# Attention and MLP on one core: the second MLP product by seven block products for a pair of token tiles

## The chip, the cores and the metric

The kernel runs on 1 core of one Trainium2 chip. The metric is device time in microseconds for one execution; the median of 3 runs of the kernel before is 604.26 us (603.35 to 604.57). Engines are named as in the profile: PE (matmul), PEld (weight load of a matmul), DVE (VectorE), ACT (ScalarE), POOL (GpSimd), SP (the queue that issues most DMAs). Lines "L674" are lines of the kernel before; "after L774" is a line of the changed one.

## What is computed

```python
def rmsnorm(x, g): return x / np.sqrt(np.mean(x * x, axis=-1, keepdims=True) + 1e-06) * g
# q, k, v: (8, 12, 448, 64)
q_n, k_n = rmsnorm(q, g_q), rmsnorm(k, g_k)
attn = softmax(q_n @ k_n^T / 8)               # per batch and head
x = concat_heads(attn @ v)                    # (8, 448, 768)
xn = (x - mean) / sqrt(var + 1e-06) * g_ln
out = x + relu(xn @ w_ch1) @ w_ch2            # 768 -> 3072 -> 768, no biases
```

## The kernel before

**Tiles.** A batch has 448 tokens. Tiles 0 to 2 hold 384 of them (128 each). The 64 tokens that are left over from two batches form one more tile, which is worked on with the odd batch. So the MLP of an even batch has three token tiles and that of an odd batch four. Activations and weights are fp16, sums fp32 in PSUM. Both weight matrices (`sh.w1`, `sh.w2`) stay in SBUF.

**The MLP** (`mlp_chunks`). The *up* product, 24 chunks of hidden features f: six matmuls (L658) of one 128x128 weight block against all the batch's tokens at once (384 or 512 columns), and one Relu on ACT (L660) into `hT[f]`. The *down* product, for every token tile and each half of the 768 output columns: 24 matmuls (L674) with a block of `hT` as the weights and 384 columns of `w2` as the moving data, in four chunks of six; then one DVE instruction (L678) multiplies by the token's 1/std (`rs`) and adds x, and the tile is stored. The last tile of the last batch takes its second half as two pieces of 192 columns. Norm scale 1/std commutes with Relu, so it is applied at the end.

**Attention** goes in 48 head pairs, 7 steps each. A step has one score matmul (L359, 448 columns; L365 for the left-over tokens), one Exp on ACT (L377) into an `E` tile, and the value matmuls (L414, L416) of the pair before. Two pairs form a *unit* (`UNITS`), whose q, k, v are loaded together (`load_unit`, L128 and L136) and prepared by `pieces`: squares on ACT (L218), their sums on DVE (L221), Ln and Exp for 1/rms (L224, L225), k times gains on POOL (`kg`, L235), its high half on ACT (`khi`, L243) and low half on DVE (`klo`, L246), q scaled on DVE (`qn`, L68), v cast on POOL (L291, L297). From unit 8 on, eight DMA transposes on SP (L264 to L277) bring k and q into `kU` and `qU`; `kU` has two buffers, so a unit's transposes wait for the last score of the unit two before.

**What sets the order.** Batch 0's attention follows the hand-written `ORDER`. From then on `run_rest` walks the MLP chunks of batch b and, after each chunk, emits as many attention steps of the next batch as its share of the cost asks for (42 steps, all done 13 chunks before the MLP's end). Inside those last 13 chunks, `ln_list` emits the next batch's layer norm: statistics, `norm` on DVE (L603), and a DMA transpose per tile on SP into `xnT` (L630). PE, ACT, POOL and SP run in this emitted order; DVE's order is chosen by the scheduler. Each engine works strictly through its own queue.

**Buffers that the change touches.** Loads: two buffers for all of q, k, v of a unit (`p_in`). Exp outputs: one buffer for an even pair (7 tiles), one for an odd pair (6) and one for the left-over tile. `xnT` and `hT` hold all 512 columns. PSUM: three banks shared by up and down (`ps_m`, tag "mlp"), two and later three for scores.

Of the kernel before, what the change touches and what calls it, by code (L numbers as in the profile page):

```python
# [55 lines left out]
RS_LO, RS_HI = 2.0 ** -2 / XS, 2.0 ** 12 / XS  # L56
# [20 lines left out]
class _Fast:  # L77


    def __init__(self, ctx, tc, sh, q, k, v, gs, g_ln, w1, w2, out):  # L80
        self.gs, self.g_ln = gs, g_ln
        self.tc, self.nc, self.sh = tc, tc.nc, sh
        self.q, self.k, self.v, self.w1, self.w2, self.out = q, k, v, w1, w2, out
        nc = tc.nc
        pool = lambda name, bufs, **kw: ctx.enter_context(tc.tile_pool(name=name, bufs=bufs, **kw))
        self.p_in = pool("p_in", 2)
        self.p_n = pool("p_n", 2)
        self.p_e = pool("p_e", 1)
# [22 lines left out]
        self.hT = fix.tile([128, NFF, 512], FP16, name="hT", tag="hT")  # L111
# [26 lines left out]
    def load_first(self):  # L138
        nc = self.nc
        flat = self.hT.rearrange("p f n -> p (f n)").bitcast(FP32)  # L140
# [29 lines left out]
    def load_unit(self, u):  # L170
        nc = self.nc
        b, hs, m = UNITS[u]
        t = self.p_in.tile([128, 3, 14, D], FP32, tag="qkv", name="qkv")
        eng = self.nc.sync if u < 11 else self.nc.gpsimd
        for n in (1, 0, 2):
            self.load_main(nc.gpsimd if u == 10 and n == 2 else eng, n, t[:, n, 0:6 * m], b, hs, 2 * m)
            self.load_left(eng, n, t[:, n, 6 * m:7 * m], b, hs, 2 * m)
        self.loads[u] = [t[:, n] for n in range(3)]
# [13 lines left out]
    def pieces(self, u):  # L192
# [9 lines left out]
        def begin():  # L202
            c["t"] = self.loads.pop(u)
            c["ssq"] = self.p_n.tile([128, 2, 14], FP32, tag="ssq", name="ssq")[:, :, 0:g]
            c["rt"] = self.p_n.tile([128, 2, 14], FP32, tag="rt", name="rt")[:, :, 0:g]
# [6 lines left out]
        def square(n):  # L212

            o = c["khl" if n == 1 else "qn"].rearrange("p g e d -> p (g e d)").bitcast(FP32)
            if u == 0 and n == 1:
                o = self.hT.rearrange("p f n -> p (f n)").bitcast(FP32)[:, 5376:5376 + g * D]
# [128 lines left out]
    def scores(self, p, i):  # L345
# [5 lines left out]
        if i == 0:  # L351
            k = 7 - p % 2
            c["E"] = self.p_e.tile([128, k, S], FP16, tag=f"E{k}", name="E")
# [17 lines left out]
        for d, x in enumerate(ps):  # L371
            if i < 6 or (p + d) % 2 == 0:
                o = c["E"][:, i]
            else:
                o = self.prs[p + d]["EL"] = self.p_e.tile([128, S], FP16, tag="EL", name="EL")
# [18 lines left out]
    def values(self, p, i):  # L394
        nc = self.nc
        c = self.prs[p]
        E = c["EL"] if i == 6 and p % 2 else c["E"][:, i]
# [95 lines left out]
    def attention(self):  # L493
# [3 lines left out]
        for u in range(4, nu):  # L497
# [4 lines left out]
            pieces = ["bai", "d", "c", "e", "j", "gv", "k", "l", "m", "w", "x", "y"]  # L502
# [5 lines left out]
            if u < nu - 2 and f"L{u + 2}" not in done:  # L508
                todo.setdefault(e + (8 if u == DMA_UNIT else 1), []).append(
                    lambda u=u: self.load_unit(u + 2))  # L510
            last = e
            for x, names in enumerate(pieces):
# [71 lines left out]
    def ln_ops(self, b):  # L584
# [14 lines left out]
        def norm(t):  # L599

            c["xn", t] = self.p_m.tile([128, DM], FP16, tag="xn", name="xn", bufs=4)
# [16 lines left out]
    def ln_list(self, b):  # L618
        ops = self.ln_ops(b)
        n = len(self.tok_tiles(b))  # L620
        call = lambda *names: lambda: [ops[x]() for x in names]
        return [call("A", "N0", "N1", "X0", "N2", "X1", *(["N3"] if n > 3 else []), "X2",
                     *(["X3"] if n > 3 else []), "R")]

    def ln_trans(self, b, xn, t):
        nc, sh = self.nc, self.sh
        if t == 0:
            self.xnT = self.p_m.tile([128, NDC, 512], FP16, tag="xnT", name="xnT")
        if b:
            nc.sync.dma_start_transpose(self.xnT[:, :, ts(t, 128)], xn)  # L630
            return
# [15 lines left out]
    def mlp_chunks(self, b):  # L647

        nc, sh = self.nc, self.sh
        tiles = self.tok_tiles(b)  # L650
        n = len(tiles)
        N = 128 * n
        xnT, hT = self.xnT, self.hT

        def up(f):
            ps = self.ps_m.tile([128, 512], FP32, tag="mlp", name="psH")
            for dc in range(NDC):
                nc.tensor.matmul(ps[:, 0:N], sh.w1[:, dc, ts(f, 128)], xnT[:, dc, 0:N],  # L658
                                 start=(dc == 0), stop=(dc == NDC - 1))
            nc.scalar.activation(out=hT[:, f, 0:N], in_=ps[:, 0:N], func=AFT.Relu)  # L660

        cur = {}
        order = [(t, g) for g in ((0, 384), (384, 384)) for t in range(n)] if b == 0 else [
            (t, g) for t in range(n) for g in (
                ((0, 384), (384, 192), (576, 192)) if (b, t) == (B - 1, n - 1)
                else ((0, 384), (384, 384)))]

        def down(t, g, s):
            cols = slice(g[0], g[0] + g[1])
            if s == 0:  # L670
                cur["ps"] = self.ps_m.tile([128, 512], FP32, tag="mlp", name="psC")
            ps = cur["ps"]
            for f in range(6 * s, 6 * s + 6):
                nc.tensor.matmul(ps[:, 0:g[1]], hT[:, f, ts(t, 128)], sh.w2[:, f, cols],  # L674
                                 start=(f == 0), stop=(f == NFF - 1))
            if s == 3:
                x = tiles[t]
                nc.vector.scalar_tensor_tensor(  # L678
                    out=x[:, cols], in0=ps[:, 0:g[1]], scalar=self.rs[:, b, t:t + 1],
                    in1=x[:, cols], op0=ALU.mult, op1=ALU.add)  # L680
                if t == n - 1:
                    self.store(b, t, cols, nc.scalar if b == B - 1 else nc.sync)
                elif cols.stop == DM:
                    self.late.append((b, t, slice(0, DM)))
            elif s == 1:
                for a in self.late:
                    self.store(*a)
                self.late = []

        for f in range(0 if b else UP_FIRST, NFF):  # L690
            yield 6 * N / 2.4, (lambda f=f: up(f))
        for t, g in order:
            for s in range(4):
                yield 6 * g[1] / 2.4, (lambda t=t, g=g, s=s: down(t, g, s))

    def up_first(self, t):
# [5 lines left out]
        for f, ps in enumerate(self.psU):  # L702
# [4 lines left out]
            if t == 2:  # L707
                nc.scalar.activation(out=self.hT[:, f, 0:384], in_=ps[:, 0:384], func=AFT.Relu)
# [26 lines left out]
    def run_rest(self):  # L735
        steps, mark, upto = self.steps, self.mark, self.upto
        tail = 13
        for b in range(B):
            chunks = list(self.mlp_chunks(b))
            total = sum(c for c, _ in chunks)  # L740
            if b + 1 == B:
                for i, (_, emit) in enumerate(chunks):
                    if i == len(chunks) - 40:
# [6 lines left out]
            done, items = 0.0, None  # L750
            for i, (cost, emit) in enumerate(chunks):
                if items and len(chunks) - i <= len(items):
                    items.pop(0)()
                emit()
                done += cost
# [9 lines left out]
    def flag(self):  # L765
# [5 lines left out]
        good = self.p_m.tile([128, n], FP32, tag="xn", name="good", bufs=4)  # L771
        cnt = self.fix.tile([128, 3], FP32, name="cnt", tag="cnt")
# [13 lines left out]
        nc.vector.tensor_reduce(out=cnt[:, 2:3], in_=good[:, 0:nr], axis=AX.X, op=ALU.add)  # L786
        nc.vector.tensor_reduce(out=cnt[:, 0:1], in_=cnt, axis=AX.X, op=ALU.add)
        ps = self.ps_o.tile([1, 1], FP32, tag="oB", name="psF")
        nc.tensor.matmul(ps, sh.ones, cnt[:, 0:1], start=True, stop=True)
        nc.vector.tensor_scalar(out=sh.flag, in0=ps, scalar1=128.0 * (n + nk + nr) - 0.5, scalar2=None,  # L790
# [3 lines left out]
def _general(tc, sh, q, k, v, g_q, g_k, out):  # L794

    nc = tc.nc
    P1, NS = 112, 4
# [108 lines left out]
def kernel(  # L906
# [19 lines left out]
    sh.warm = const.tile([128, 1], FP32, name="warm")  # L926
# [5 lines left out]
    sh.gmax = const.tile([128, 1], FP32, name="gmax")  # L932
# [13 lines left out]
    with tc.If(val > 0, label="general"):  # L946
        _general(tc, sh, q, k, v, g_q, g_k, out)
# [30 lines left out]
```

## Time and profile before

| what | us |
|---|---|
| median of 3 runs | 604.26 |
| the profiled execution, device time | 604.66 |
| its span | 603.0 |
| PE busy | 577.6 |
| ACT / DVE / POOL busy | 358.5 / 287.8 / 184.8 |
| first matmul / start of the last matmul, from the span's start | 5.26 / 598.81 |
| MLP of batch 1: first up, first down, end | 123.0, 162.8, 200.0 |
| MLP of batch 2: first up, first down, end | 200.0, 232.9, 261.6 |
| MLP of batch 7: first up, first down | 536.3, 567.6 |

The span is the time from the first to the last recorded instruction; the device time is 1.7 us longer. A matmul's own duration in the profile includes its way through the array, and the next one starts long before it ends, so costs on PE are read here from the spacing of starts: a run of matmuls in the chain of work divided by their number. Granted clock is 0.996 over the span and 1.00 in every later stage, so spacings of different stages can be compared.

### The profile page before, as it was taken

How to read it: one execution, taken by the hardware profiler on the slowest of the kernel's cores; microseconds unless marked ns; L12 is line 12 of the kernel's file. 1: busy time of each engine (PE TensorE's matmuls, PEld its weight loads, DVE VectorE, ACT ScalarE, POOL GpSimd, SP SyncE). 2: the span in 40 equal slices, each digit the busy share in tenths (PEclk: the TensorE clock that was granted, in tenths of full speed). 3: DMA queues.
4: the chain of work that ended last, by engine and by line, in shares of the span. 5: the costliest groups of instructions: out<-in, count | busy, mean ns of one | idle time of the engine just before them, and what ended most of it. 6: DMA issues, size and time to landing. Idle time of an engine off the chain costs nothing.

```text
span 603.0 us, 11494 instructions
## 1 busy us (share of the span) xinstructions
PE 577.6 (96%) x4502; PEld 341.9 (57%) x4502; DVE 287.8 (48%) x645; ACT 358.5 (59%) x673; POOL 184.8 (31%) x246
## 2 busy tenths in 40 slices
PE   2877999999999999999999999999999999999997
PEld 1555566654566666655566666655556666654565
DVE  5798567734256255724256255642355422450011
ACT  5996887359743598548755498537765287114300
POOL 3844432232642345423542245505322000000000
PEclk9899999999999999999999999999999999999999
DMA  7999999574957578947866386848533330040011
GB/s 209 281 196 206 207 222 197 106 212 86 146 130 125 106 126 155 170 121 122 120 127 131 104 125 153 165 120 152 114 68 88 92 62 1 27 106 1 1 53 54
DMA packets 130285, 75.18 MB, mean 125 GB/s; under 512 B 96500, under 2 KB 120420, under 8 KB 130228
## 3 DMA queue, kind: packets, MB, share of 16 engines
q1 hardware_dynamic: 113092, 44.50, 37.7%
q0 software_dynamic: 16192, 29.30, 22.9%
q8 instruction: 36, 0.59, 0.4%
q10 hardware_dynamic: 944, 0.62, 0.3%
q14 instruction: 21, 0.17, 0.1%
HBM read 52.30 MB, written 11.01 MB: 105 GB/s over the span
## 4 chain that ended last, share of the span: by engine, by line
PE 88%; ACT 2%; DVE 2%; issue 0%; DVEq 0%
PE psC L674 36%; PE psH L658 35%; PE psS L359 8%; PE oA L414 5%; PE oB L416 2%; PE psS L365 1%; ACT E L377 1%; PE tr L322 0%; ACT khl L218 0%; PE psU L704 0%; DVE stat L582 0%; ACT hT L660 0%; PE tr L336 0%; DVE xn L603 0%; DVE x L431 0%
## 5 line engine op out<-in xcount | busy, mean ns | idle before, releaser
L658 PE MATMUL psH<-xnT,w 128*128 128x512 f16 (+1 forms) x1134 | 242.1, 353 | 0.0
L674 PE MATMUL psC<-w,hT 128*128 128x384 f16 (+1 forms) x1368 | 234.8, 324 | 0.0
L377 ACT ACTIVATE E<-psS,rr_all 128x448 f16<-128x448 f32 x312 | 193.5, 635 | 49.5 <-PE psS L359 48.6
L660 ACT ACTIVATE hT<-psH 128x512 f16<-128x512 f32 (+1 forms) x189 | 104.0, 550 | 130.9 <-PE psH L658 128.8
L674 PEld LDWEIGHTS <-hT 128*128 128x128 f16 x1368 | 127.2, 98 | 78.8 <-issue 4.3
L658 PEld LDWEIGHTS <-w 128*128 128x128 f16 x1134 | 102.3, 98 | 83.3 <-issue 2.9
L359 PE MATMUL psS<-qU,kU 128*128 128x448 f16 x288 | 101.3, 358 | 8.7 <-ACT E L377 5.8
L414 PEld LDWEIGHTS <-E 128*128 128x128 f16 x936 | 65.0, 99 | 44.3 <-issue 5.0
L235 POOL TENSOR_TENSOR qkv<-qkv,gprod 128x896 f32<-128x896 f32 x21 | 43.7, 2079 | 95.8 <-issue 51.7
L414 PE MATMUL oA<-v,E 128*128 128x65 f16 x864 | 66.9, 194 | 0.1
L678 DVE SCALAR_TENSOR_TENSOR x<-psC,rs_all,x 128x384 f32<-128x384 f32 x48 | 29.2, 616 | 78.4 <-PE psC L674 77.9
L128 POOL DMA_DIRECT2D qkv<-in_k_dram x14 | 11.1, 793 | 137.0 <-ACT E L377 64.3
L416 PE MATMUL oB<-v,E 128*128 128x65 f16 x288 | 52.1, 194 | 0.1
L429 DVE RECIPROCAL rec_all<-oA 128x6 f32<-128x6 f32 x48 | 9.3, 194 | 88.2 <-PE oA L414 87.8
L221 DVE TENSOR_REDUCE ssq<-khl 128x14 f32<-128x896 f32 (+1 forms) x24 | 25.6, 1065 | 44.6 <-ACT khl L218 44.5
L359 PEld LDWEIGHTS <-kU 128*128 128x128 f16 x288 | 28.2, 99 | 25.9 <-issue 6.0
L221 DVE TENSOR_REDUCE ssq<-qn 128x14 f32<-128x896 f32 (+1 forms) x25 | 26.2, 1046 | 21.8 <-ACT qn L218 21.7
L68 DVE SCALAR_TENSOR_TENSOR qn<-qkv,rr_all 128x256 f16<-128x256 f32 (+1 forms) x72 | 26.4, 426 | 18.1 <-ACT rr_all L225 18.1
L416 PEld LDWEIGHTS <-E 128*128 128x128 f16 x312 | 30.3, 97 | 0.2 <-DVE xl L436 0.2
L431 DVE TENSOR_TENSOR x<-oA,rec_all 128x384 f32<-128x384 f32 x48 | 26.8, 558 | 1.5
L582 DVE BATCH_NORM_STATS2 stat<-x 128x6 f32<-128x256 f32 (+1 forms) x75 | 26.0, 404 | 0.6
L246 DVE TENSOR_TENSOR khl<-qkv,khl 128x896 f16<-128x896 f32 x21 | 22.7, 1079 | 4.0 <-ACT khl L243 3.9
(114 smaller groups left out, 447.3 us busy)
## 6 DMA issues: line engine op xcount, KB each, us to landing
out_dram<-x SPq DMA_DIRECT2D x20, 384.0 KB, 2.5
qkv<-in_v_dram POOLq DMA_DIRECT2D x15, 384.0 KB, 6.5
qkv<-in_k_dram POOLq DMA_DIRECT2D x14, 384.0 KB, 3.9
qkv<-in_q_dram POOLq DMA_DIRECT2D x14, 384.0 KB, 5.4
w<-in_moe_w_ch_dram POOLq DMA_DIRECT2D x3, 1536.0 KB, 13.0
w<-in_moe_w_ch_dram POOLq DMA_DIRECT2D x2, 2304.0 KB, 24.8
qkv<-in_k_dram SPq DMA_DIRECT2D x7, 384.0 KB, 5.7
qkv<-in_q_dram SPq DMA_DIRECT2D x7, 384.0 KB, 6.0
```

The lines of the kernel that those rows point to most:

```text
L68: nc.vector.scalar_tensor_tensor(out=out, in0=x, scalar=8.0, in1=r.unsqueeze(2).broadcast_to([x.shape[0], g, D]), op0=ALU.mult, op1=ALU.mult)
L221: nc.vector.tensor_reduce(out=c["ssq"][:, n], in_=c["sq", n], axis=AX.X, op=ALU.add)
L235: (nc.vector if u in DVE_KG else nc.gpsimd).tensor_tensor(out=c["t"][1], in0=c["t"][1], in1=sh.gprod.unsqueeze(1).broadcast_to([128, g, D] ...
L359: nc.tensor.matmul(ps[0][:, 0:S], c["main"][:, ts(i, 128)], c["q"][:, ts(h, S)], start=True, stop=True)
L377: nc.scalar.activation(out=o, in_=x[:, 0:S], func=AFT.Exp, scale=self.units[u][3][:, g:g + 1], bias=EXP_BIAS)
L414: nc.tensor.matmul(oA[:, t, cs], E[:, ts(t, 128)], rhs, start=(i == 0 and t == 0), stop=(i == 6 and t == 2))
L416: nc.tensor.matmul(oB[:, cs], E[:, 320:448], rhs, start=(i == 0), stop=(i == 6))
L431: nc.vector.tensor_tensor(out=x[:, :, 128 * hp:128 * hp + 128].rearrange("p t (e d) -> p t e d", e=2), in0=oA[:, :, :, 0:D], in1=rec[:, 0: ...
L658: nc.tensor.matmul(ps[:, 0:N], sh.w1[:, dc, ts(f, 128)], xnT[:, dc, 0:N], start=(dc == 0), stop=(dc == NDC - 1))
L660: nc.scalar.activation(out=hT[:, f, 0:N], in_=ps[:, 0:N], func=AFT.Relu)
L674: nc.tensor.matmul(ps[:, 0:g[1]], hT[:, f, ts(t, 128)], sh.w2[:, f, cols], start=(f == 0), stop=(f == NFF - 1))
L678: nc.vector.scalar_tensor_tensor(out=x[:, cols], in0=ps[:, 0:g[1]], scalar=self.rs[:, b, t:t + 1], in1=x[:, cols], op0=ALU.mult, op1=ALU.add)
```

## The change

**Down product.** Batch 0 keeps the plain product. From batch 1 on, tiles are taken in *groups*: pairs [0,1] and [2,3] in odd batches, [2] and then [0,1] in even ones. For a pair, the down product is a 2x2 block product (two token tiles; two halves of f; two halves of the output columns), done in the Strassen-Winograd form: seven products of 12 matmuls with 384 columns, numbered "1" to "7", in place of eight. DVE makes the sums of `hT` blocks: three instructions of 512 fp16 elements for every four f and their partners (`sums`), and one of 1536. The sums of weight blocks (`w2s`, T1, T2, T4) are made once on DVE, beside the end of batch 0 and the start of batch 1, and T3 = B12 - B22 replaces B12 in `w2`; a single tile uses T3 too, with one more sum. Partial results go to x by more DVE adds (`add`), by a copy of product 1 to SBUF on ACT, and, except in batch 7, by three ACT multiplications with `rs` and three POOL additions (`join`).

**Up product.** It runs per group too: 256 columns for a pair (two f share a PSUM bank and a Relu), 128 for a single tile (four f). `xnT` holds one group, in one buffer: the second group's transposes are emitted once the first group's up product has been.

**Loads and exp tiles.** q, k and v have one buffer each; the next unit's k, q or v is loaded as soon as the present unit's `klo`, `qn` or left-over v cast has read its own. Units 5 and 7 are loaded into idle parts of other buffers. `khi` and `klo` move ahead of q's square in `pieces`. Exp tiles come from one ring of 9.

**Safety.** The final check (`flag`) tests also that the scales of two tiles of a pair are within a factor of 4; otherwise the general path runs, which loads half of `w2` again.

```diff
-        self.p_in = pool("p_in", 2)
+        self.p_in = pool("p_in", 1)
...
+        t = self.loads.setdefault(u, [None] * 3)
+        for n in which:
+            t[n] = flat[:, n] if flat is not None else self.p_in.tile(
+                [128, 14, D], FP32, tag="qkv"[n], name="qkv"[n])
...
-            pieces = ["bai", "d", "c", "e", "j", "gv", "k", "l", "m", "w", "x", "y"]
+            pieces = (["bai", "d", "c", "e", "j", "gv", "k", "l", "m", "w", "x", "y"]
+                      if u <= DMA_UNIT else
+                      ["bai", "d", "j", "k", "c", "e", "gv", "l", "m", "w", "x", "y"])
...
+                for y in set(names) & set("klw"):
+                    if DMA_UNIT <= u < nu - 1:
+                        todo.setdefault(at + 1, []).append(
+                            lambda u=u, t={"k": 1, "l": 0, "w": 2}[y]: self.load_unit(u + 1, (t,)))
...
-            c["xn", t] = self.p_m.tile([128, DM], FP16, tag="xn", name="xn", bufs=4)
+            c["xn", t] = self.p_m.tile([128, DM], FP16, tag="xn", name="xn", bufs=2)
...
+            if t in (0, 2):
+                self.xnT = self.p_m.tile([128, NDC, 256], FP16, tag="xnT", name="xnT")
+            nc.sync.dma_start_transpose(self.xnT[:, :, ts(t % 2, 128)], xn)
...
+    def mlp_group(self, b, tiles, end):
...
+        def up(f):
+            ps = self.ps_m.tile([128, k, N], FP32, tag="mlp", name="psH")
+            for i in range(k):
+                for dc in range(NDC):
+                    nc.tensor.matmul(ps[:, i], sh.w1[:, dc, ts(f + i, 128)], self.xnT[:, dc, 0:N],
+                                     start=(i == 0 and dc == 0), stop=(i == k - 1 and dc == NDC - 1))
+            nc.scalar.activation(out=hT[:, f:f + k], in_=ps, func=AFT.Relu)
...
+        def sums(i):
+            f, f2 = slice(4 * i, 4 * i + 4), slice(HALF + 4 * i, HALF + 4 * i + 4)
+            if n == 1:
+                tt(S1[:, f], A1(f), A1(f2), ALU.add)
+                return
+            tt(S1[:, f], A2(f), A2(f2), ALU.add)
+            tt(S2[:, f], S1[:, f], A1(f))
+            tt(A2(f), A2(f), A1(f))
...
+        p = run("1", A1(lo), B11)
+        yield p[0]
+        yield 0, lambda: sums(2)
+        yield p[1]
+        yield add("1", 0, 0)
+        yield from run("2", A1(hi), B21)
+        yield add("2", 0, 0)
+        yield 0, lambda: tt(A1(hi), A1(hi), S2)
+        yield late
+        yield from run("6", S2, T2)
+        p = run("5", S1, T1)
+        yield p[0]
+        yield 0, lambda: nc.scalar.copy(out=U, in_=bank["1"])
+        yield p[1]
+        yield 0, lambda: tt(U, U, bank["6"], ALU.add)
+        yield 0, lambda: tt(V, U, bank["5"], ALU.add)
...
+        yield from run("7", A2(lo), T3)
+        yield add("7", 1, 1)
+        yield add("7", 1, 0)
+        if not last:
+            for out, x, t in ((U, U, 1), (W, V, 0), (V, V, 1)):
+                yield 0, lambda out=out, x=x, t=t: nc.scalar.activation(
+                    out, x, AFT.Copy, scale=self.rs[:, b, t0 + t:t0 + t + 1])
+            yield join(V, 1, 1)
...
+        yield from run("3", A1(hi), B22)
...
+            yield from run("4", A2(hi), T4)
...
+        for i, x in enumerate(self.mlp_group(b, first, False)):
+            yield x
+            if i % 2 and i // 2 < len(second):
+                yield 0, ln[f"N{second[i // 2]}"]
+            if i == ups - 1:
+                for t in second:
+                    yield 0, ln[f"X{t}"]
+        yield from self.mlp_group(b, second, True)
+
+    def groups(self, b):
+        return ([0, 1], [2, 3]) if b % 2 else ([2], [0, 1])
```

More of the change, by code (lines that the diff above doesn't have):

```diff
@@ L507, in attention @@
                 continue
[L508 to L510 removed]
+            if u == DMA_UNIT - 2:
+                todo.setdefault(e + 1, []).append(lambda u=u: self.load_unit(u + 2))
             last = e
@@ L657, in up @@
             for dc in range(NDC):
-                nc.tensor.matmul(ps[:, 0:N], sh.w1[:, dc, ts(f, 128)], xnT[:, dc, 0:N],
+                nc.tensor.matmul(ps[:, 0:384], sh.w1[:, dc, ts(f, 128)], xnT[:, dc],
                                  start=(dc == 0), stop=(dc == NDC - 1))
-            nc.scalar.activation(out=hT[:, f, 0:N], in_=ps[:, 0:N], func=AFT.Relu)
+            nc.scalar.activation(out=hT[:, f], in_=ps[:, 0:384], func=AFT.Relu)
         cur = {}
[L663 to L666, printed above, removed]
@@ L690, in mlp_chunks @@
[L690 to L694, printed above, removed]
+                self.add(0, t, g, ps)
+                if g and t < 2:
+                    self.late.append((0, t, slice(0, DM)))
+                elif t == 2:
+                    self.store(0, t, slice(g * HCOL, g * HCOL + HCOL))
+            elif s == 1:
+                self.store_late()
@@ new lines, in first_mlp, with store_late, add @@
+        for f in range(UP_FIRST, NFF):
+            yield 6 * 384 / 2.4, (lambda f=f: up(f))
+        for g in range(2):
+            for t in range(3):
+                for s in range(4):
+                    yield 6 * HCOL / 2.4, (lambda t=t, g=g, s=s: down(t, g, s))
+    def store_late(self):
+        for a in self.late:
+            self.store(*a)
+        self.late = []
+    def add(self, b, t, g, ps, c0=0, c1=HCOL):
+        x = self.tok_tiles(b)[t][:, g * HCOL + c0:g * HCOL + c1]
+        self.nc.vector.scalar_tensor_tensor(
+            out=x, in0=ps, scalar=self.rs[:, b, t:t + 1], in1=x, op0=ALU.mult, op1=ALU.add)
@@ L754, in run_rest @@
                 emit()
+                if cost and (i > 33 if b == 0 else b == 1) and ops:
+                    ops.pop(0)()
                 done += cost
```

214 lines of the change are left out of this document (156 added, 58 removed).

## The prediction

> **What bounds the kernel now.** I read the page's busy shares first, then the stretches of single batches, then PE's waits, and last the chain of work in order of time. In the stretch table (columns: stretch; total us; busy us of PE, PEld, DVE, ACT, POOL; clock; DMA share; GB/s) the rows are batch 2 up to the end of its attention steps, its last 13 chunks, and then the waits of PE after 100 us:
>
> ```profile
> PE 577.6 (96%) x4502; PEld 341.9 (57%) x4502; DVE 287.8 (48%) x645; ACT 358.5 (59%) x673; POOL 184.8 (31%) x246
> ```
> ```profile
> 199.96:248.93 48.97, 48.79 (x428) 30.33 (x427) 24.73 (x60) 40.19 (x79) 27.34 (x37) 1.00 0.79 141
> 248.93:261.55 12.62, 12.62 (x80) 7.58 (x79) 9.00 (x18) 2.14 (x5) 0.69 (x3) 1.00 0.73 153
> ```
> ```profile
> PE psS L359 <- ACT E L377: 0.4, 2, 0.2
> ```
>
> PE is busy throughout at full clock, and after 100 us it waits 0.4 us for others in all. So after 100 us the time is what PE is given, and a matmul's price is its spacing. The chain in order of time (start, us, what) gives spacings from unbroken runs:
>
> ```profile
> 55.81 2.01 PE psU L704 x36
> 110.40 12.78 PE psC L674 x78
> 540.49 27.30 PE psH L658 x126
> 567.79 31.27 PE psC L674 x216
> ```
>
> 128 columns: 2.01/36 = 55.8 ns, each matmul with a weight load of its own. 384 columns: 12.78/78 = 163.8 ns. 512 columns: 27.30/126 = 216.7 ns. These lie on a line of 0.419 ns a column, which gives 109.4 ns for 256 columns, a width that the trace does not show. The last row fits too: its 48 matmuls of 192 columns leave 83 ns each.
>
> **PE's work, step by step.** The built order gives the counts. Batch 0 is unchanged.
> 1. Up, batches 1 to 7. Before: 576 x 216.7 + 432 x 163.8 = 195.6 us. After: 11 pairs x 144 = 1584 of 256 columns, 173.3 us, and 3 single tiles x 144 = 432 of 128 columns, 24.1 us: 197.4. Cost 1.8 us.
> 2. Down. A pair needs 84 matmuls in place of 96; 11 x 12 = 132 fewer x 163.8 ns = 21.6 us gained. Single tiles keep 48. The last pieces of 192 columns stay.
> 3. Scores, values and transposes keep their counts.
> Net -19.8 us. From the profiled execution's 604.66 this gives 584.9, if nothing new waits. That execution is 0.4 us above the median of the runs, so 584.5 is the floor beside the median.
>
> A weight load reads 98 ns as a mean, but in the psU run 36 of them pass at 55.8 ns each, so I price short matmuls by spacing. The Trainium skill speaks against the narrow up product: the page TensorE: Matmul & The Clock Gate, Back-to-back issue gap, puts a sustained stream of weight loads and matmuls at about 81 ns for 128 columns. By that figure the single tiles would cost 432 x 25 ns = 10.9 us more; the psU row, at 55.8 ns with weight loads, is against it, and it stays out of the sum.
>
> **Work beside PE.** None of these is on the path while the engine keeps up.
> 4. ACT. Relus: 150 of 512 columns at 600 ns = 90 us in place of 93.5. New: 11 copies and 27 scalings of 384 columns; an xnT copy of 384 columns took 0.48 us, so 38 x 0.48 = 18 us. 358 becomes 373 of 585 us.
> 5. DVE. An fp16 sum of two fp16 tiles is not in the trace. From above: `klo`, the only wide two-input SBUF form, took 618 ns at 448 and 1075 at 896 elements, so 683 ns at 512, 1.73 us at 1536, 1.34 us at 1152. From below: an fp16 copy of 896 took 393 ns, so no less than some 0.25 us at 512. I take the upper price, from the row that is nearest in form. A pair then adds 9 x 0.68 + 1.73 + four more adds x 0.616 = 10.3 us, a single tile 2.0, the 16 weight sums 21 us: 11 x 10.3 + 6 + 21 = 140. DVE goes from 288 to 428 of 585 us, 73%. Batch 2's stretch above has 33.7 us of DVE work in 61.6; with 12.3 more it is at 46 in 60.
> 6. POOL. 27 additions of 384 elements at 2079 x 384/896 = 0.89 us: 24 us more, 209 of 585. `load_unit` of units 9 and 10 leaves SP for POOL, nine issues of 0.60 to 0.80 us each.
> 7. Buffers. In `ORDER`, the values that free each of the nine ring tiles stand ahead of the score that wants it, on PE's own queue; no new wait, 0. The first 100 us, where most of the present waits are, keep their path.
>
> The Trainium skill, VectorE: DVE Perf Modes, gives fp16 tensor_tensor two elements a cycle at 0.96 GHz (section on auto-detection); an estimate from it is 0.27 us plus the fixed part for 512, about 40% under item 5. No row here shows it; it changes no term below.
>
> **New waits, and what hides them.**
> 8. The second group's transposes. They follow the eight transposes of a unit on SP, which is in order. In an odd batch there is room: the unit's transposes are released by step 5 and SP is free before the first group's up product ends; two transposes need 1.24 + 2.8 us (issue, landing) against 13.8 us of products. In an even batch it is tight. SP before, batch 2:
>
> ```profile
> 206.77 2.63 SPq L264 DMA_TRANSPOSE kU<-khl  x1
> 209.45 4.76 SPq L267 DMA_TRANSPOSE kU<-khl  x2
> 214.31 3.83 SPq L274 DMA_TRANSPOSE qU<-qn  x3
> 218.19 2.51 SPq L277 DMA_TRANSPOSE qU<-qn  x2
> ```
> The start is 6.8 us after the batch's first matmul, the end 13.9 us later; in batches 4 and 6 it took 12.5 and 11.6, at best anywhere 10.6. After: step 5 is emitted behind four up chunks (24 x 55.8 = 1.34 us each; a step costs one score of 0.19 and four values of 0.03, 0.31 us), so release is at 4 x 1.34 + 5 x 0.31 + 0.2 = 7.1 us, SP is free at 17.7 to 21.0, and the second transpose has landed 4.0 us later, at 21.7 to 25.0. PE reaches the pair's up product after 6 x 1.34 + 8 x 0.98 + 20 x 0.31 = 22.1 us. Wait 0 to 2.9 us in each of three batches; I take 1.2, a unit between the best and batch 6: **+3.6 us** (0 to 8.7).
> 9. Product "6" reads S2. Between the last up matmul and it lie 24 matmuls, 3.9 us. Needed: Relu 0.60 and two sums 1.37. That leaves 1.9 us for DVE's queue. In DVE's built order a square sum (L221, 1.08 us) that waits for ACT stands between these two sums in the first pair of odd batches. So the wait is 0 mostly, up to 1.1 us; I take 0.2 x 11 pairs = **+2.2 us** (0 to 12). PSUM banks: each is freed one product (1.97 us) or more ahead of its next use, against an add of 0.62; 0.
> 10. `khi` now follows `kg` by two steps, and POOL may still issue loads: an even batch's unit has about 15 us, in which POOL has 9.6 us of own work and waits for `qn`. ACT may then stand up to 2 us, with Exps and Relus queued behind it; three score banks and three up banks let PE run on for about that long. I take 0; it is the start of rival C.
>
> Sum: 604.66 - 19.8 + 3.6 + 2.2 = 590.7; beside the median 590.3. A difference under 0.2% (1.2 us) is what a measurement of this kernel cannot tell from no change.
>
> **The rivals.**
> A. All is hidden: 584.5. For it: PE's 0.4 us of waits now, and the room in items 4 to 6. Against: item 8's tight sum. Chance 0.22.
> B. DVE's queue holds up most pairs: each pays 0.7 to 1.1 us at product "6", "7" or the next bank, 8 to 12 us: 598 to 602, with item 8 in it. For it: 46 us of 60 in even batches, in one order. Chance 0.14.
> C. Slower: the single load buffer. k's load now waits for `klo`, and the next unit's chain for the load. The ring is load 2.0 us of issue and 3.9 of landing, `kg` 2.08, `khi` 0.96, `klo` 1.08: 10.0 us of the 15 us that an even unit has; odd units have 20. Each of four hand-overs waits behind what its queue holds (POOL for `qn`, ACT and DVE about 1 us each). If these waits pass 5 us the unit's transposes are late and PE stands at the scores. It decides against the change once each of the 9 even units loses (604.3 - 590.3)/9 = 1.6 us; at 2 us each 608. Against it: the chain has 11 steps between `klo` and the transposes' release. Chance 0.09.
> D. Short matmuls are held by their weight loads: at 98 ns, the PEld mean, for 128 columns, 432 x 42 ns = 18 us more, 608. The skill's rule above goes this way, at 81 ns: 601. Against: the psU row. Chance 0.03.
> E. The change does nothing that shows: the order has 1212 down matmuls (in units of 384 columns) against 1344, so it does what it says, and E needs gains and waits to cancel: 604. Chance 0.02.
>
> **How the numbers follow.** The forecast, 590.3, has the remaining 0.50; its own range is 585.5 to 597 (items 8 and 9 from near 0 to two thirds of their bounds). Leaving out C, D, E (0.14) and a little of B's upper edge, the range is 584.3 to 602. Faster: forecast, A, B: 0.86. Same: 0.02. Slower: C and D, 0.12.
>
> **What would show it.** Right: the row of down products with 84 matmuls a pair at 163 ns; up matmuls spaced by 109 and 56 ns; PE waits after 100 us of some 6 us, xnT transposes as the releaser in batches 2, 4 and 6, DVE sums next. Wrong: spacing above 60 ns at 128 columns (D); scores waiting on `kU` or `qU` landings (C); PE waits on DVE spread over all pairs (B); a lower granted clock, for which there is no sign here.

## The result, and the profile after

| | before | after |
|---|---|---|
| median of the runs, us | 603.81 (603.29 to 604.57) | 623.54 (622.34 to 626.30) |
| profiled execution: span, us | 603.0 | 622.6 |
| TensorE's mean granted clock | 0.996 | 0.988 |

The change made the kernel slower: ratio 1.033, interval 1.029 to 1.037. The forecast was 590.3, range 584.3 to 602.0.

First the busy shares of the changed kernel, then batch 2 in two rows as before (its group of one tile and most of the pair's up product, then the pair's product; columns as in the prediction's stretch table):

```profile
PE 566.5 (91%) x5366; PEld 410.8 (66%) x5366; DVE 385.3 (62%) x834; ACT 375.7 (60%) x693; POOL 223.0 (36%) x288
```
```profile
209.24:257.92 48.68, 45.50 (x541) 36.16 (x540) 26.34 (x65) 36.65 (x68) 25.65 (x37) 1.00 0.76 147
257.92:278.19 20.27, 16.82 (x103) 9.50 (x100) 15.75 (x30) 7.45 (x14) 5.52 (x6) 0.92 0.41 90
```

PE's share fell from 96 to 91%. Batch 2 took 68.95 us in place of 61.59; PE is idle for 6.6 us of it, and in the second row the clock is below 1. Compare the 0.4 us that PE waited after 100 us before with its waits after 100 us now (who waited, for whom; total us, times, longest):

```profile
PE ps L774 <- ACT hS L826: 7.4, 3, 2.7
PE psS L377 <- ACT E L387: 5.0, 6, 1.1
PE psH L741 <- DMA xnT<-xn: 4.2, 3, 1.7
PE psH L741 <- DVE x L709: 1.7, 2, 1.3
```

Smaller ones bring the sum to 21.3 us. PE's own prices are those of the prediction. Unbroken runs of up products (chain in order of time; start, us, what):

```profile
218.38 1.35 PE psH L741 x24
...
588.46 15.72 PE psH L741 x144
```

256 columns: 15.72/144 = 109.2 ns (predicted 109.4). 128 columns: 1.35/24 = 56 ns (55.8). The 1056 full down matmuls have a median spacing of 162 ns. So the work did shrink by about the 19.8 us of the prediction's net, and the kernel lost 39 us elsewhere. The starts of the batches' first up matmuls show where. "Work" is the prediction's items 1 and 2 for that batch (a pair -1.97, the up product +0.2 or +0.3); loss is change less work:

| batch | before, us | after, us | change | work | loss |
|---|---|---|---|---|---|
| 0 (to 123.02, to 133.11) | 123.02 | 133.11 | +10.1 | 0 | 10.1 |
| 1 | 76.94 | 76.13 | -0.8 | -3.6 | 2.8 |
| 2 | 61.59 | 68.95 | +7.4 | -1.8 | 9.1 |
| 3 | 76.65 | 73.79 | -2.9 | -3.6 | 0.8 |
| 4 | 61.59 | 66.96 | +5.4 | -1.8 | 7.1 |
| 5 | 76.65 | 74.29 | -2.4 | -3.6 | 1.3 |
| 6 | 59.89 | 65.47 | +5.6 | -1.8 | 7.4 |
| 7, to the end | 66.67 | 63.9 | -2.8 | -3.6 | 0.9 |

The losses add to 39.5 us. They sit in batch 0 and in the even batches, at few places, not in every pair.

**Batch 0.** The chain around 90 to 100 us of the changed kernel (start, us, what), and the same 18 us of it as a stretch:

```profile
77.65 18.05 DMA w<-in_moe_w_ch_dram
...
95.73 0.04 DVE w2s L715
...
96.41 2.09 DVE w2s L715 x3
...
98.53 0.66 DVE kU L339
```
```profile
85.00:103.00 18.00, 9.29 (x81) 5.86 (x79) 8.19 (x14) 6.19 (x13) 2.63 (x2) 0.81 0.67 105
```

Four weight sums (L715) stand in VectorE's order ahead of the copy that frees `tr` (L339). VectorE's order is chosen by a scheduler in this part of the program, and it moved them there. The first sum waits for the second half of w2, which lands at 95.7 us; VectorE stands 9.7 us, PE 8.8 us, and the granted clock is 0.50 from 95.1 to 101.9 us, past the end of PE's stand.

**Even batches.** The chain into the stand of 2.5 us in batch 2:

```profile
262.96 1.41 DVE stat L597 x4
264.37 0.42 DVE stat L612 x3
264.79 1.79 DVE xn L618 x2
...
266.61 0.62 DVE x L709
267.23 0.88 DVE hS L746
...
268.18 0.49 ACT hS L826
...
268.71 6.39 PE ps L774 x28
```

PE finished product 6 at 266.2 us and wants a PSUM bank for product 5. In the built order of these three pairs its wait is for ScalarE's copy of U out of the bank of product 1 (L826); in the other eight pairs product 5 is given the bank of product 2 and waits for an add (L709). (The expectations of e2 and e4 below name this stand by product 7; it is ahead of product 5.) U is written over S2, so the copy waits for the big difference that reads S2 (L746); that waits its turn behind the add of product 1 (L709), and the add stands behind 3.6 us of the next batch's statistics and norms (L597, L612, L618). The bank of product 2 would have come free no sooner: its add started at 268.01 us, behind the difference, and took 0.61, and the copy was done at 268.66. Stands are given in this text by the spacing of PE's starts: 2.5, 2.5 and 2.9 us in the three batches. The waits view says 2.3, 2.3 and 2.7, because it counts from the modelled end of the last matmul.

My first theory had four places: weight sums ahead of the kU copy (about 10 us), the bank of product 5 (8 us and half clock), ScalarE standing for `kg` ahead of `khi` (5 to 8 us), and the transposes behind a unit's on SP (4.2 us). The rivals were that groups or single load buffers cost by themselves, that VectorE's load costs everywhere, and that stands would only move when one is taken away.

### The profile page after: what moved, and what is told of

The parts are those of the page before. It is cut to its first block, busy times and chain, and to the rows that moved or that the text cites. A ratio compares the mean times of both kernels' runs of the same rounds, so it can differ in the third digit from the quotient of the medians.

```text
span 622.6 us, 13600 instructions
## 1 busy us (share of the span) xinstructions
PE 566.5 (91%) x5366; PEld 410.8 (66%) x5366; DVE 385.3 (62%) x834; ACT 375.7 (60%) x693; POOL 223.0 (36%) x288
## 4 chain that ended last, share of the span: by engine, by line
PE 58%; DMA 12%; DVE 11%; issue 4%; ACT 4%; SPq 2%; POOL 1%; ACTq 0%; DVEq 0%; POOLq 0%
PE psH L741 27%; PE ps L774 20%; PE psS L371 5%; DMA q<-in_q_dram 4%; PE oA L424 3%; DMA w<-in_moe_w_ch_dram 3%; DMA xnT<-xn 2%; ACT E L387 2%; DMA kU<-khl 2%; DVE stat L597 2%; DVE khl L261 1%; DVE hS L746 1%; DVE xn L618 1%; DVE x L709 1%; PE oB L426 1%
## 5 line engine op out<-in xcount | busy, mean ns | idle before, releaser
L741 PE MATMUL psH<-xnT,w 128*128 128x256 f16 (+1 forms) x2016 | 218.1, 261 | 6.0 <-DMA xnT<-xn 4.2
L741 PEld LDWEIGHTS <-w 128*128 128x128 f16 x2016 | 174.0, 98 | 26.8 <-issue 5.1
L743 ACT ACTIVATE hS<-psH 128x512 f16<-128x512 f32 x150 | 89.8, 598 | 110.3 <-PE psH L741 109.6
L774 PEld LDWEIGHTS <-hS 128*128 128x128 f16 x1080 | 101.9, 99 | 74.3 <-issue 15.6
L774 PE MATMUL ps<-w,hS 128*128 128x384 f16 x672 | 120.5, 327 | 0.0
L746 DVE TENSOR_TENSOR hS<-hS 128x512 f16<-128x512 f16 (+1 forms) x119 | 58.9, 517 | 57.4 <-ACT hS L743 55.8
L774 PE MATMUL ps<-w2s,hS 128*128 128x384 f16 (+1 forms) x408 | 73.4, 330 | 8.3 <-ACT hS L826 7.4
L250 POOL TENSOR_TENSOR k<-k,gprod 128x896 f32<-128x896 f32 x19 | 40.0, 2106 | 56.4 <-ACT khl L233 33.2
L709 DVE SCALAR_TENSOR_TENSOR x<-ps,rs_all,x 128x384 f32<-128x384 f32 x60 | 36.2, 615 | 26.9 <-PE ps L774 26.2
L71 DVE SCALAR_TENSOR_TENSOR qn<-q,rr_all 128x256 f16<-128x256 f32 (+1 forms) x70 | 24.4, 406 | 31.7 <-ACT rr_all L240 20.4
```

The lines of the kernel that those rows point to most:

```text
L250: (nc.vector if u in DVE_KG else nc.gpsimd).tensor_tensor(out=c["t"][1], in0=c["t"][1], in1=sh.gprod.unsqueeze(1).broadcast_to([128, g, D] ...
L709: self.nc.vector.scalar_tensor_tensor(out=x, in0=ps, scalar=self.rs[:, b, t:t + 1], in1=x, op0=ALU.mult, op1=ALU.add)
L741: nc.tensor.matmul(ps[:, i], sh.w1[:, dc, ts(f + i, 128)], self.xnT[:, dc, 0:N], start=(i == 0 and dc == 0), stop=(i == k - 1 and dc == ND ...
L743: nc.scalar.activation(out=hT[:, f:f + k], in_=ps, func=AFT.Relu)
L746: nc.vector.tensor_tensor(out=out, in0=a, in1=c, op=op)
L774: nc.tensor.matmul(bank[x][:, c], a[:, f], w[:, f, c], start=(start and f == 0), stop=(stop and f == HALF - 1))
```

## The experiments

Each run is compared with 603.8 us for the kernel before and 623.5 for the changed kernel.

**e1: weight sums behind the second add of batch 0.** Each chunk's first sum gets a true dependency:

```diff
+        late = lambda f: nc.vector.tensor_copy(out=w2s[0:1, 0, f, 0:1],
+                                               in_=self.xs[0][0:1, 1, 0:3].unsqueeze(2))
         for c in range(4):
+            ops += [lambda f=f: late(f)]
```

> The twelve first weight sums get a true dependency on the second add of batch 0 (a copy of three elements of x into the place that each chunk's first sum overwrites), so that VectorE's order can no longer put them ahead of the copy of kU; nothing else is changed, 4 tiny copies of about 0.06 us are added. Theory 'sum ahead of the copy': the 9.7 us that VectorE stands for the second half of w2, the 8.8 us that TensorE stands for the kU copy at 90.4 us and the half clock behind it (6.83 us at half clock, about 3.4 us lost) go, against the time of 623.5 us: 611 to 615 us, batch 0's first down product at about 91.5 instead of 99.9 us. Rival 'DMA': batch 0 is late because the second half of w2 lands only at 95.7 us, and the down products themselves would wait for it: then TensorE's wait only moves to the first down product (or its second half), and the time falls by 4 us or less, to 619 us or more. Rival 'vector work in general': VectorE's 16 sums are only moved to 105 to 140 us and delay adds and bank releases there: 618 us or more.

Measured 610.93 us (609.92 to 611.23), 12.6 below the changed kernel. The same 18 us, of e1:

```profile
85.00:103.00 18.00, 17.94 (x174) 11.75 (x173) 12.34 (x30) 13.11 (x24) 6.52 (x8) 1.00 0.84 142
```

PE went from 9.29 to 17.94 us busy. The theory holds and "DMA" falls: PE never waits for w2's second half itself. In the profiled execution batch 0 returned 9.9 us (the first up product of batch 1 starts at 123.20 in place of 133.11). Another 2.2 came in batch 2, whose stand of 2.5 us was not followed by half clock this time.

**e2: U over the dead low half of A1, not over S2.**

```diff
+        UT, same = U, lambda x: x
+        if n == 2 and not last:
+            UT = self.hS.rearrange("p f n -> p (f n)")[:, 0:NFF * 256].bitcast(FP32).rearrange(
+                "p (f n) -> p f n", n=128)[:, 0:6, 0:64]
+            same = r6
...
-        yield 0, lambda: nc.scalar.copy(out=U, in_=bank["1"])
+        yield 0, lambda: nc.scalar.copy(out=UT, in_=same(bank["1"]))
```

> U, the partial sum that ScalarE copies out of the bank of product 1, is put where the low half of A1 lay (dead after product 1) instead of over S2; so the copy no longer has to wait for the big difference A1(hi) - S2 that reads S2. Only the last batch keeps the old place. Theory 'bank of product 1': the 2.5, 2.5 and 2.9 us that TensorE stands ahead of product 7 in batches 2, 4 and 6 go, with the half clock behind two of them (3.41 us at half clock each, about 1.7 us lost each): 7.9 + 3.4 = 11 us, to 612 to 615 us; the clock's extra drops at 269 and 549 us are gone. Rival 'the big difference itself': product 3 reads A1(hi) - S2 and would then wait for the same late difference, one product (1.97 us) later: the gain is then at most 3 x 2 us, to 617 us or more, and a wait of about 0.5 to 1 us stands at product 3.

Measured 617.63 us (617.43 to 619.25): 5.9 less, half of what I expected. The time is the rival's (617 or more), but its mechanism is not there: no wait stands ahead of product 3 in batches 2, 4 and 6. Here is PE's wait ahead of product 5 in e2, to be held against the 7.4 us above:

```profile
PE ps L774 <- ACT hS L832: 4.6, 3, 1.8
```

The copy now waits for the add of product 1, in place of the difference one step behind it. So the overlay was the last 0.9 us of each stand. The rest is VectorE's queue ahead of that add. (The time also gained because the clock did not fall at 269 and 549 us.)

**e3: order of the pieces as before.**

```diff
-    ["bai", "d", "j", "k", "c", "e", "gv", "l", "m", "w", "x", "y"]
+    ["bai", "d", "c", "e", "j", "k", "gv", "l", "m", "w", "x", "y"]
```

> The pieces of preparing a unit stand in the order of the kernel before again (square and total of q ahead of khi and klo) for the units past the first ones, so khi comes two pieces later behind kg. Theory 'ScalarE stands for kg': the waits of ScalarE for kg on POOL (2.5 us at a time in batch 2) and TensorE's waits at the scores behind them (0.76 + 0.98 + 0.55 us and 1.3 us in each of the batches 2, 4 and 6, some 8 us in all without the waits for the transposes) shrink by more than half: 616 to 619 us. Rival 'single load buffer': k's buffer comes free two pieces later, its load is issued and lands later, and the next unit's prep, kU and qU are late: 623 us or more, with DMA waits at k's square or kg, up to the 608 + 20 = 628 us of my prediction's case C on top of the loss. Rival 'E ring': the waits at the scores come from the exp ring of nine buffers and stay as they are: 622 to 625 us.

Measured 622.13 us (620.08 to 624.22), above the 616 to 619 of the theory and not told from the changed kernel by these runs. The waits did what the theory says, at L377 from 5.0 to 1.5 us, but the transposes' wait grew from 4.2 to 5.1 and the stand at the kU copy from 8.9 to 9.8. A cause was shown, its price was not.

**e4: in even batches the pair first.** `([2], [0, 1])` became `([0, 1], [2])`.

> In the even batches the pair of tiles goes first and the single tile second, so the single's one transpose instead of the pair's two stands in the second place, and the pair's Strassen chain is no longer the batch's end. Theory 'where the tail stands': the big difference no longer competes with the next batch's statistics and norms, so the stands of 2.5 us ahead of product 7 go (7.9 us and 3.4 us of half clock), and the stands for the second group's transposes (1.3 to 1.8 us in each of three batches) shrink or go: 608 to 614 us. Rival 'place changes nothing': VectorE's load is the same, and the adds and the two joins on POOL now meet the next group's up products: the stands move to the second group's first up product, 618 us or more. Rival 'no single cause': within 2 us of 623.5.

Measured 643.8 us (642.69 to 646.56), and it settles nothing: with the single tile last, the next batch's transposes are issued before its up product is through, and in the built order 72 of its 144 up matmuls read the next batch's `xnT`, so part of the computation was changed. PE then stood 20.8 us for xnT in three batches.

**e5: the groups, with eight plain block products.** No sums, weight sums, U, V or joins.

```diff
+        for t in range(n):
+            for g in range(2):
+                yield from run(x, a(lo), w2[:, lo, ts(g, HCOL)], stop=False)
+                yield from run(x, a(hi), w2[:, hi, ts(g, HCOL)], start=False)
+                yield add(x, t, g)
```

> The groups, the small buffers, the exp ring and the order of the pieces stay; the down product is done by eight plain block products, without sums, weight sums, U, V and joins (the outputs are the reference's). Theory 'the saving is real and is eaten by stands': the 132 matmuls come back (+19.8 us net of the narrow ups' +1.8), the stand for w2 and its half clock go (12.6 us by the run that moved the sums) and those ahead of product 5 go (9.3 us by their sum); what stays are the scores' waits (about 7.7 us), the transposes' (about 3.6 us) and the narrow ups: 603.8 + 1.8 + 7.7 + 3.6 = 617 us, 614 to 620. Rival 'groups cost nothing, Strassen's vector work costs it all': 604 to 608 us. Rival 'single load buffer and groups are the loss': over 622 us.

Measured 614.07 us (613.45 to 614.48), ratio to before 1.0165 (1.0151 to 1.018). The two largest of PE's waits after 100 us:

```profile
PE psH L741 <- DMA xnT<-xn: 4.7, 3, 1.8
PE psS L377 <- ACT E L387: 1.7, 3, 0.6
```

So the groups, with the single load buffers and the ring of exp tiles, cost 10 us by themselves, most of it transposes, scores and narrow ups. The transposes' stands are no part of Strassen's method, and of the scores' 5.0 us 3.3 come with it.

**e6: e1, e2 and e3 together.**

> The edits of the first three runs together (weight sums behind the second add, U over the low half of A1, order of the pieces as before). If the three causes are separate places their gains add: 623.5 - 12.6 - 5.9 - 1.4 = 603.6 us, 601 to 606. If they share cover (a stand that goes only moves to the next one), 607 us or more. The half-clock stretches at 95, 269 and 549 us are all gone, and TensorE's remaining waits are the transposes' (about 4 to 5 us in all) and 1.6 to 2 us ahead of product 5 in each even batch.

Measured 607.08 us, from 603.74 to 609.40. The median is past the 601 to 606 of separate places and just inside the rival's 607 or more. The profiled execution, at 603.74 us the shortest of the four, has no half clock at 95, 269 and 549 us and a mean clock of 0.999; the other three have 0.991 to 0.997. The stands of 1.6 to 2.3 us ahead of product 5 and 4.8 us for transposes stay.

**e7: e1, and the norms 4 us earlier.** The last attention steps of each batch, the aggregate and the norms move ahead of the pair's last up products; the transposes stay behind them.

```diff
-        tail = 13
+        tail = 17
-        return [lambda: [ops[x]() for x in ("A", *(f"N{t}" for t in first),
-                                            *(f"X{t}" for t in first), "R")]]
+        return [lambda: [ops[x]() for x in ("A", *(f"N{t}" for t in first), "R")],
+                lambda: [ops[f"X{t}"]() for t in first]]
-                if items and len(chunks) - i <= len(items):
+                if items and len(chunks) - i <= (24 if b == 0 else 34):
```

> With the weight sums behind the second add as in the first run (610.9 us), the last attention steps of a batch and with them the next batch's aggregate and norms are put 4 us earlier (a tail of 17 instead of 13 units of 0.96 us), so that on VectorE they stand ahead of the last up products' sums and not ahead of the add of product 1; the transposes of the first group keep their place behind the last up. U stays where it was. Theory 'product 5's bank waits for add 1, the big difference and U's copy, because VectorE stands 5 us in statistics and norms there': the stands of 2.5, 2.5 and 2.9 us and the three of 0.5 us go, 9.3 us and some half clock: 600 to 603 us. Rival 'VectorE is simply full at the batch's end': the sums then come late instead, TensorE waits at product 6 or 5 for S2 or S1 by as much: 609 us or more. Rival 'ScalarE': the denser attention steps make the scores' waits grow by more than the gain: 606 us or more.

Measured 604.07 us (602.24 to 607.30), 6.9 under e1 and just past the 600 to 603 of the theory. PE's wait for the U copy fell from 7.4 to 0.9 us, and 2.2 us remain for adds:

```profile
PE ps L776 <- DVE x L709: 2.2, 5, 0.8
PE ps L776 <- ACT hS L828: 0.9, 1, 0.9
```

So it was VectorE's queue at the batch's end, not VectorE's load: the same work stands earlier and the sums are not late. The rest of the expected gain went to stands of 2.0, 1.44 and 1.44 us at 60, 77 and 94 us, beside batch 0.

**e8: e7 with e2 and e3.**

> All four edits together. By separate places: 610.9 - 9.3 (bank of product 5) - 3.5 (the part of the scores' waits that the order of pieces took away) = 598 us, 595 to 601, which would be faster than the kernel before by 0.5 to 1.4 per cent; the transposes' waits of 1 to 2 us in each even batch stay. If TensorE's stands only move, 604 us or more, no gain over the kernel before.

Measured 606.51 us (604.10 to 612.98), no gain. The waits of ScalarE after 100 us in the profiled execution (610.59 us) name a new one; behind it is the same wait in e6:

```profile
ACT qn L233 <- DMA q<-in_q_dram: 9.0, 4, 4.8
```
```profile
ACT qn L233 <- DMA q<-in_q_dram: 0.7, 1, 0.7
```

With the old order of pieces, q's square comes early; with one load buffer, q's load was issued at 364 to 366 us and took 10 us to land; ScalarE stood until 375.5 for it, with the exps behind it, and PE at the scores for 4.9 us. This is rival C's mechanism, for q. It came only with e7's earlier steps: e3 and e6 have the same order of pieces and the same single buffers, and 0.6 and 0.7 us of this wait.

**e9: e7, batch 0 with its old tail.** `tail = 17 if b else 13`.

> As the run with the norms early (weight sums behind the second add, tail of 17), but batch 0 keeps its tail of 13. In that run TensorE stood 2.0 + 1.44 + 1.44 us at 60, 77 and 94 us where it stood 1.0 + 0.45 us before; if that came from the denser attention steps beside batch 0, about 3 us come back: 601 us, 599 to 602.5. Rival: these stands have another cause, or only move: 603.5 us or more.

Measured 600.09 us (599.64 to 604.79), ratio to before 0.994 (0.9927 to 0.9953). The stands at 60 to 94 us are back at 1.0 and 0.4.

**e10: e9, `khi` one piece later, q's pieces where the change put them.**

```diff
-    ["bai", "d", "j", "k", "c", "e", "gv", "l", "m", "w", "x", "y"]
+    ["bai", "d", "", "jk", "c", "e", "gv", "l", "m", "w", "x", "y"]
```

> As e9, and khi stands one piece later, together with klo, so three pieces behind kg, while q's square and total keep their late place, and k's buffer is freed no later. The stands at the scores that hang on ScalarE's stand for kg (1.24, 0.87, 0.55 and 1.15 us in each of two batches of the run with the norms early, 7.6 us in all) fall by half or more: 3 to 5 us below e9, 596 to 598.5 us, which would beat the kernel before by about 1 per cent. Rival 'kg is late anyway': klo then comes late on VectorE and kU and qU behind it; no gain over e9, or a loss.

Measured 598.12 us (597.25 to 601.26). ScalarE's wait for `kg`, first in the changed kernel, then in e10:

```profile
ACT khl L258 <- POOL k L250: 10.4, 10, 1.6
```
```profile
ACT khl L258 <- POOL k L250: 1.8, 3, 0.6
```

The stands at L377 are gone. The gain over e9 is 2.0 us, less than the 3 to 5 expected, and the two kernels' runs overlap; in place of the old stands are 2.3 us at other scores.

**e11: e10 with U as in e2.**

> As e10, with U over the low half of A1. The 1.0 us stands ahead of a product in batches 2, 4 and 6 that the run with the norms early kept (they end with U's copy or an add) shrink: 0 to 3 us below e10. Rival: the copy into the strided place changes nothing, since the copy waits for the add of product 1 now: the same as e10 within 1 us.

Measured 596.48 us (594.98 to 603.36), ratio to before 0.9908 (0.9873 to 0.9944): the fastest version, 0.9% faster than the kernel before. The 1.6 us under e10 are not shown, since the runs of the two overlap widely. Its page, and all of PE's waits after 100 us:

```profile
PE 560.9 (95%) x5366; PEld 407.6 (69%) x5366; DVE 382.7 (65%) x838; ACT 374.8 (63%) x693; POOL 223.1 (38%) x288
```
```profile
PE psS L371 <- ACT E L387: 2.6, 2, 1.3
PE psH L743 <- DVE x L709: 1.4, 1, 1.4
PE ps L776 <- DVE hS L748: 1.3, 5, 0.3
PE psH L743 <- DMA xnT<-xn: 0.2, 1, 0.2
```

VectorE is as busy as in the changed kernel, 383 us against 385, and PE waits 5.5 us in place of 21. No arithmetic was taken away: only the order of instructions and one overlay differ.

**e12: e11's order with the plain products of e5.**

> The mended order (tail of 17 past batch 0, norms ahead of the transposes, khi one piece later) with the eight plain products of e5 in place of Strassen's seven; no sums, no weight sums. Against e11 (596.5 us) it tells what Strassen alone is worth once the stands are gone. If the 132 matmuls are saved in full and the vector work lies beside the product: 596.5 + 21.6 - about 2 us (U, joins and the weight sums' stand of 1.6 us) = 614 to 618 us. If the mends help the plain products as well, the stands of e5 (4.7 us for transposes, 1.7 us at the scores) go from its 614.1: 607 to 610 us, and Strassen is worth 11 to 13 us of its 21.6. Rival: the mends help only Strassen, 613 to 615.

Measured 611.90 us (611.00 to 612.86). This lies between the ranges I had given (607 to 610, and 613 or more). In the mended order Strassen's method is worth 611.9 - 596.5 = 15.4 us of the 21.6; in the change's own order it cost 623.5 - 614.1 = 9.4. The mends give the plain version 2.2 us. About 3 of the missing 6 us lie ahead of batch 2, where the weight sums are made: there e11 is 0.9 us ahead of e12 (198.33 against 199.24 us), and two pairs should have given 3.9.

## Why the prediction was wrong

- **Items 1 to 3, net -19.8: right.** 109.2, 56 and 162 ns per matmul against 109.4, 55.8 and 163.8, with the counts of the order. Rival D falls, and with it the 81 ns that the Trainium skill (TensorE: Matmul & The Clock Gate, Back-to-back issue gap) gives at 128 columns: this trace has 56, each matmul with its weight load.
- **Items 5 and 7 failed: "None of these is on the path while the engine keeps up" and "The first 100 us ... keep their path".** I priced the 16 weight sums as load (21 us; at a measured 0.75 us each they are 12) and never asked what the first of them waits for and what is queued behind it. The built order has four of them ahead of the kU copy, and the profile of before has the landing time of w2's halves, the other part of the answer. Taking the sums from that place was worth 12.6 us (e1). In the row of the kernel before, 24.8 us is the median of the two halves' landings; the second half, issued at 78.39 us, took 26.0 and landed at 104.4:

```profile
w<-in_moe_w_ch_dram POOLq DMA_DIRECT2D x2, 2304.0 KB, 24.8
```

- **Item 9 failed in its last sentence: "each is freed one product (1.97 us) or more ahead of its next use, against an add of 0.62; 0".** The add was compared with its own length, not with the queue that it stands in. At the end of an even batch that queue is 3.6 us of statistics and norms, and the order behind it is add, difference, copy. Before the change PE had no such wait: the same norms hid behind down products of 24 matmuls, 3.9 us, and three banks; now a product is half as long. 7.4 us of waits in the trace and half clock behind two of them; moving the norms returned 6.9 us (e7 against e1), the overlay of U alone 5.9 (e2 against the changed kernel). Rival B named "the next bank" and a delay in most pairs; the delay is 2.5 us, but in three pairs of eleven.
- **Item 9's main term, 2.2 us for S2's sums at product 6: not there.** No stand ahead of product 6 shows in the waits. The upper price of 683 ns for a sum of 512 was also too high: the trace has a median of 0.42 us, and 0.95 for 1536. The estimate by the Trainium skill (VectorE: DVE Perf Modes, auto-detection), two elements a cycle, 0.27 us plus a fixed part, agrees with it: 1024 elements more take 0.53 us, which is what two a cycle at 0.96 GHz give. VectorE's 428 us came out as 385.
- **Item 10 failed: "I take 0".** ScalarE stood 10.4 us for `kg`; PE stood 5.0 us at the scores. Three score banks did not cover it. The part that comes with Strassen is 3.3 us (e5), and putting `khi` one piece later removed it (e10). ScalarE's own stand for `kg` is nearly as long without Strassen (8.9 us in e5); why PE felt it less there is not shown.
- **Item 8: the mechanism was right, the size partly luck.** Predicted 3.6 us, by the transposes of batches 2, 4 and 6; measured 4.2, with the longest 1.7. In batch 2 SP was free 20.6 us after the batch's start (at 229.86 us), inside the 17.7 to 21.0:

```profile
227.35 2.51 SPq L292 DMA_TRANSPOSE qU<-qn  x2
229.96 2.56 SPq L644 DMA_TRANSPOSE xnT<-xn  x2
```

  But the 1.2 us chosen for a batch does not follow from its own words: a unit between the best and batch 6 gives 0 to 0.6. The second transpose landed 24.8, 24.5 and 24.0 us after the three batches' starts, and PE came at 23.4, 23.4 and 22.4 in place of 22.1. On time, it would have stood about 7 us.
- **Rival C** did not decide the changed kernel: ScalarE's waits for loads there are 0.9 us. Its mechanism shows in e8, for q (9.0 us; at most 2.1 in any other run). The order of pieces that was to avoid it, with `khi` early, brought item 10's stand.
- **Two slips of the working change nothing.** With 163.8 ns for the other 168 matmuls the row of 216 leaves 78 ns, not 83, for those of 192 columns (the trace has 83, beside 162.6). Two thirds of the bounds of items 8 and 9 give 598, not 597.

Of the 39 us, 8.8 are PE's stand in batch 0 and 21 its waits after 100 us. The half clock accounts for 4.6: 2.7, 3.4 and 3.0 us of work at half speed in the three stretches, each costing half of its length. That leaves about 5 that I did not place. The runs of e6, e8 and e11 scatter by 6 to 9 us, where those of the kernel before keep within 1.6. The granted clock can explain a part: e11 took 603.36 us at 0.991 and 594.98 at 1.000, and 0.9% of the span is 5.4 us. Which stands bring that about is open, since one execution of each kernel was profiled.

## What to carry to other kernels

An instruction moved beside the bound engine costs what it makes the next one in its queue wait, not its own length: for each added instruction read from the built order what stands behind it, and from the trace when its last input lands. When a step on the bound engine is halved, the time in which its buffers must come free is halved too; compare it with the whole queue ahead of the releasing instruction, in the stage where that queue is longest. Where the gain in work is real and the time is worse, mend the order first: here the same arithmetic took 623.5 us and 596.5.

## What the runs showed of the hardware

A stand of PE can cost more than its length. The clock in the profile's rows, around the stand of batch 0 and behind that of batch 2 in the changed kernel:

```profile
95.08:101.91 6.83, 2.67 (x14) 1.63 (x14) 6.12 (x10) 0.00 (x0) 0.00 (x0) 0.50 0.02 4
269.15:272.56 3.41, 3.41 (x13) 1.65 (x11) 2.23 (x4) 0.00 (x0) 0.00 (x0) 0.50 0.38 127
```

In the second row 384 columns take 0.32 us each in place of 0.16. The half-clock stretches between 90 us and the kernel's last 5 us were 3.41, 6.83 or 10.24 us long in all profiled executions. Stands of 5 us and more each brought one; of the stands of 2.5, 2.5 and 2.9 us in the changed kernel the first and the last were followed by one, and of the same three in e1 only the last. One stand of 2.3 us was followed by one too, in e4. The profiled executions without a stand above 2.4 us had none. The Trainium skill (TensorE: Matmul & The Clock Gate, What's actually happening) has a free-running window of some 3.4 us, and the lengths agree with it. That stands shorter than this window are sometimes followed by half clock is shown by these traces alone.
